# Casting the second half of the slot outputs on DVE, and an idle fill moved behind a product

## The chip, the core and the metric

The kernel runs on one core of one Trainium2 chip. A core has a matrix engine (TensorE, in the profile PE for its products and PEld for its weight loads), a vector engine (DVE), a scalar engine (ACT), GpSimd (POOL) and a sync engine (SP) that issues most transfers here. The engines run their own queues in order and wait for one another through semaphores. The metric is the device time of one execution in microseconds (us), and lower is better.

## The reference, cut to what matters

Sliding-window attention feeds a soft mixture of experts, and that one's output feeds a second mixture in which every token goes to one expert:

```python
attn = softmax(scale * q @ k.T, banded: 0 <= i - j < 64)
x = attn @ v                                  # 2304 tokens, 512 wide
logits = x @ phi                              # 32 slots, 4 for each of 8 experts
slot_input = softmax(logits, tokens).T @ x
slot_out[e] = relu(slot_input[e] @ w1[e]) @ w2[e]
x = softmax(logits, slots) @ slot_out
idx = argmax(cosine(x, expert_emb) / tau)     # one of 8 for each token
out[t] = gate[t] * (relu(x[t] @ w1b[idx[t]]) @ w2b[idx[t]])
```

## The kernel before

The program has four stages. Attention runs over 32 half head pairs (up to about 126 us in the trace). Then the 32 slots are finished, and their two layers run over the eight experts' weights (`layer1`, lines 707 to 711, and `layer2`, lines 726 to 730). Then the kernel finds which expert the first token goes to, loads that expert's weights from memory, and builds the routing values. The last stage, `ffn`, is the second mixture's two products for all tokens (172 to 283 us).

The change touches the seam between the second and the fourth stage. `layer2` leaves the 32 slot outputs in `so_ps`, one PSUM tile of 128 x 512 f32, which is one PSUM bank. Three copies read it: lines 843 and 844 cast its left and right 256 columns to bf16 into `sob`, and line 845 copies all of it to `so` in f32. All three stand on ACT.

From `sob` goes a short chain. Line 880 multiplies it, in four pieces of 128 columns, by `c0`, the first token's slot weights. Line 881 (DVE) copies the result to `k0b`. After three transposes (line 796, `trT(9)`) line 885 multiplies `k0b` by the expert embeddings, lines 886 and 887 (DVE) find the largest, and line 888 has SP load its number. With it `load_e` (lines 890 to 896) issues ten transfers, in turn a part of the expert's first matrix `w1e` and of its second `w2e`; the first part of `w1e` is 256 KB. From `so` line 903 makes a second set of products, whose results `esT` feed line 912 and so `gst`.

The copies of combining weights (`combT`, through `split_rows`, lines 697 to 703) write a rounded part `hi` on ACT and a rest on DVE.

The order of the work at the head of `ffn` is written out by hand in the string `SEQ` (line 9), one letter a step: `g` is `logits2` (line 923, six products of six token tiles each), `f` is `fill(still, 1)` (line 113), a product of the identity with itself into a PSUM tile that nobody reads, `U` is the step `u_part` (line 999, the first product with `w1e`; its result goes through `split_rows` into `ust`), `V` splits a part of `w2e` on DVE (lines 1031 and 1032) and `Q` is `up` for a block of 256 tokens (line 1019), which needs `ust`. Each engine gets its instructions in the order in which this string writes them.

Of the kernel before, what the change touches and what calls it, by code (L numbers as in the profile page):

```python
# [7 lines left out]

SEQ = 'ggfUgffVQPU2WR1PW0U3RQ0S1U3LP2SQWUL1Q3S0WPK23P2Q10ORGM012R3R'
FP32 = mybir.dt.float32  # L10
F32R = mybir.dt.float32r
BF16 = mybir.dt.bfloat16
# [7 lines left out]
def tile_kernel(ctx, tc, q, k, v, phi, w1, w2, emb, tau, w1b, w2b, out):  # L20
    nc = tc.nc
# [20 lines left out]
    def ps(tag):  # L42
        return pp.tile([128, 512], FP32, tag=tag, name=tag)
# [55 lines left out]
    with tc.manual_schedule():  # L99
# [580 lines left out]
        sob = cpool.tile([128, DM], BF16, name="sob")  # L680
# [144 lines left out]
        so_ps = ps("pv")  # L825
# [15 lines left out]
            layer2(t)  # L841
        pT = trT(6)
        nc.scalar.copy(out=sob[:, 0:256], in_=so_ps[:, 0:256])
        nc.scalar.copy(out=sob[:, 256:512], in_=so_ps[:, 256:512])
        nc.scalar.copy(out=so, in_=so_ps)
        mctx.close()

# [140 lines left out]
        def ffn(first):  # L988
# [26 lines left out]
            def up(nb, f0, n=2, dve=False):  # L1015
                a, l = hbuf[nb % 3]
                p = ps("s")[:, 0:256 * n]
                for i in range(n):
                    nc.tensor.matmul(p[:, 256 * i:256 * i + 256], lhsT=ucol[f0 + i], rhs=cTs[:, 256 * NBS[nb]:256 * NBS[nb] + 256], start=True, stop=True)  # L1019
                av = a[:, f0:f0 + n, :].rearrange("p f n -> p (f n)")  # L1020
                if dve:
                    nc.vector.tensor_scalar(out=av, in0=p, scalar1=0.0, scalar2=None, op0=ALU.max)
                else:
                    nc.scalar.activation(out=av, in_=p, func=ACTF.Relu)  # L1024
                nc.vector.scalar_tensor_tensor(out=l[:, f0:f0 + n, :].rearrange("p f n -> p (f n)"), in0=p, scalar=0.0,  # L1025
                                               in1=av.bitcast(FP32), op0=ALU.max, op1=ALU.subtract)
# [52 lines left out]
            def gates_now():  # L1079
# [6 lines left out]
                "P": lambda n: up(0, *CH[n]), "Q": lambda n: up(1, *CH[n]), "R": lambda n: up(2, *CH[n])}  # L1086
            for x in SEQ:
                if x in "0123":
# [65 lines left out]
```

## Time and profile before

| what | value |
|---|---|
| time, median of 3 runs | 291.96 us (291.24 to 292.74) |
| the profiled execution's own time | 290.68 us |
| its span in the trace | 289.0 us |
| TensorE products busy | 270.9 us, 94% |
| DVE / ACT / POOL busy | 169.4 / 123.7 / 60.4 us |
| chain of waits that ended last | PE 73%, ACT 9%, DVE 7%, DMA 3% of the span |
| mean granted TensorE clock | 0.995 |

The span is what the trace covers; the time also has what lies around it, 1.68 us here. A busy share says little by itself: what counts at a place is the chain of waits, which names for each stretch the engine that nobody else was waiting for.

### The profile page before, as it was taken

To read this page: it belongs to the slowest core of one execution; us is meant where nothing else is said; L and a number is where in the kernel's file an instruction comes from. 1 tells how busy PE (TensorE), PEld (TensorE's weight loads), DVE (VectorE), ACT (ScalarE), POOL (GpSimd) and SP (SyncE) were. 2 spreads that over 40 slices of the span, in tenths; PEclk is the share of its full clock that TensorE was granted. 3 is DMA by queue.
4 is the path that set the end of the run, shared out by engine and by line. 5 is a ranking of instruction groups with operands and counts; after the bars stand their busy time and mean duration, and the time that the engine had idled before them with its cause. 6 is when DMAs were issued, how large, how long until landed. Compare 5 with 4: busy or idle time off the path is not lost.

```text
span 289.0 us, 7506 instructions
## 1 busy us (share of the span) xinstructions
PE 270.9 (94%) x2846; PEld 209.0 (72%) x2846; DVE 169.4 (59%) x670; ACT 123.7 (43%) x328; POOL 60.4 (21%) x135
## 2 busy tenths in 40 slices
PE   7699989999989899899999999999999999999991
PEld 6477768877868787663342596788888888888891
DVE  4679877888778777553860256988333423233210
ACT  3785876687667867551310353324212112211100
POOL 5556434351423332003200005330000000000000
PEclk9999999999999999999999999999999999999998
DMA  5999999989999999999999089002220111010111
GB/s 134 282 226 282 280 280 285 297 255 282 271 335 277 283 299 334 387 366 385 390 387 344 6 229 354 3 0 92 81 47 36 39 61 49 36 39 36 74 43 35
DMA packets 53657, 57.23 MB, mean 198 GB/s; under 512 B 21490, under 2 KB 34034, under 8 KB 53618
## 3 DMA queue, kind: packets, MB, share of 16 engines
q1 hardware_dynamic: 53472, 56.70, 62.3%
q8 instruction: 24, 0.39, 0.6%
q14 instruction: 15, 0.12, 0.1%
q10 hardware_dynamic: 146, 0.02, 0.0%
HBM read 51.99 MB, written 4.72 MB: 196 GB/s over the span
## 4 chain that ended last, share of the span: by engine, by line
PE 73%; ACT 9%; DVE 7%; DMA 3%; SPq 2%; issue 2%; POOL 1%; POOLq 0%; ACTq 0%
PE et L1047 17%; PE pv L1047 17%; PE pv L325 5%; PE pv L729 5%; ACT sm L279 4%; PE tr L217 4%; PE s L1019 3%; PE tr L710 3%; PE s L710 2%; PE et L292 2%; ACT ets L298 2%; PE pv L382 2%; PE s L262 2%; DMA v<-in_v_dram 2%; DVE sm L278 2%
## 5 line engine op out<-in xcount | busy, mean ns | idle before, releaser
L279 ACT ACTIVATE sm<-sm,nm 128x128 f32<-128x128 f32 x144 | 47.3, 391 | 23.7 <-DVE nm L278 23.5
L1024 ACT ACTIVATE h<-s 128x512 fp32r<-128x512 f32 (+1 forms) x39 | 21.8, 565 | 68.7 <-PE s L1019 68.7
L1025 DVE SCALAR_TENSOR_TENSOR h<-s,h 128x512 fp32r<-128x512 f32 (+1 forms) x39 | 25.0, 648 | 40.0 <-ACT h L1024 39.9
L278 DVE CUSTOM_DVE_ANT_0 sm<-s,mask 128x128 f32<-128x128 f32 x144 | 34.1, 286 | 11.2 <-PE s L268 6.6
L1047 PE MATMUL et<-w2h,h 128*128 128x512 f32 (+1 forms) x160 | 37.4, 372 | 0.0
L1047 PE MATMUL pv<-w2h,h 128*128 128x512 f32 x144 | 36.8, 392 | 0.0
L1047 PEld LDWEIGHTS et<-w2h,h 128*128 128x128 f32 x160 | 27.1, 189 | 5.4 <-issue 0.8
L325 PE MATMUL pv<-v,ets 128*64 128x65 f32 x640 | 25.7, 226 | 4.6 <-ACT ets L298 3.3
L1047 PEld LDWEIGHTS pv<-w2h,h 128*128 128x128 f32 x144 | 26.1, 188 | 4.6
L325 PEld LDWEIGHTS pv<-v,ets 128*64 128x64 f32 x640 | 21.4, 137 | 11.1 <-ACT ets L298 8.2
L217 PE MATMUL tr<-ident,spare 128*128 128x128 f32 x120 | 19.4, 285 | 1.9 <-POOL spare L212 1.8
L186 POOL COPY v<-v 64x512 f32<-64x512 f32 x16 | 9.7, 609 | 51.3 <-DMA v<-in_v_dram 51.2
L298 ACT COPY ets<-et 128x512 f32<-128x512 f32 x32 | 18.3, 573 | 4.2 <-PE et L292 3.7
L212 POOL COPY spare<-spare 128x512 f32<-128x512 f32 x30 | 18.4, 613 | 8.1 <-PE tr L217 5.1
L1047 PE MATMUL et<-w2l,h 128*128 128x512 f32 (+1 forms) x80 | 19.4, 368 | 0.0
L292 PE MATMUL et<-ident,sm 128*128 128x128 f32 x128 | 19.3, 273 | 0.0
L1047 PE MATMUL pv<-w2l,h 128*128 128x512 f32 x72 | 19.1, 390 | 0.0
L312 DVE COPY xT<-tr 128x320 f32<-128x320 f32 (+1 forms) x31 | 14.0, 451 | 4.3 <-ACT ets L300 3.6
L337 DVE TENSOR_TENSOR x<-pv,rc 128x256 f32<-128x256 f32 (+1 forms) x32 | 15.7, 491 | 1.1
L217 PEld LDWEIGHTS tr<-ident,spare 128*128 128x128 f32 x120 | 12.6, 140 | 4.1 <-POOL spare L212 2.2
L1019 PEld LDWEIGHTS s<-cTs,ust 128*128 128x128 f32 x72 | 13.5, 190 | 2.8
L1047 PEld LDWEIGHTS et<-w2l,h 128*128 128x128 f32 x80 | 13.7, 189 | 2.1
(309 smaller groups left out, 432.5 us busy)
## 6 DMA issues: line engine op xcount, KB each, us to landing
w<-in_moe_w_dram SPq DMA_DIRECT2D x32, 1024.0 KB, 7.8
v<-in_v_dram SPq DMA_DIRECT2D x32, 128.0 KB, 4.8
spare<-in_q_dram SPq DMA_DIRECT2D x15, 256.0 KB, 7.2
spare<-in_k_dram SPq DMA_DIRECT2D x15, 256.0 KB, 6.4
out_dram<-acc SPq DMA_DIRECT2D x15, 256.0 KB, 2.0
w1e<-in_moe_w_dram SPq DMA_DIRECT2D x3, 512.0 KB
w2e<-in_moe_w_dram SPq DMA_DIRECT2D x3, 512.0 KB, 8.0
out_dram<-acc SPq DMA_DIRECT2D x6, 128.0 KB, 2.0
```

What stands on the lines that cost most here:

```text
L212: g.tensor_copy(out=perm[nm], in_=t)
L217: nc.tensor.transpose(po[:, r], perm[nm][:, r].rearrange("p h d -> p (h d)"), ident)
L278: nc.vector.tensor_tensor_reduce(out=sm[:, u], in0=s[h][:, a], in1=m, scale=-scale, scalar=3.0e38, op0=ALU.add, op1=ALU.min, accum_out=nm[ ...
L279: nc.scalar.activation(out=sm[:, u], in_=sm[:, u], func=ACTF.Exp, bias=nm[:, u:u + 1], scale=-1.0)
L292: nc.tensor.transpose(p[:, 128 * u:128 * u + 128], e[:, u, :], ident)
L298: nc.scalar.copy(out=o[:, 0:4], in_=p.rearrange("p (n h q) -> p n h q", n=4, h=2))
L325: nc.tensor.matmul(p[64 * par:64 * par + 64, a, h, :], lhsT=et[:, u, x, :], rhs=vt[:, sl, h, :], start=True, stop=True)
L337: nc.vector.tensor_tensor(out=x_tok[b, hp][:, js[0]:js[0] + nj].rearrange("p j (h d) -> p j h d", h=2), in0=p[:, :, :, 0:64], in1=rc[:, 0: ...
L1019: nc.tensor.matmul(p[:, 256 * i:256 * i + 256], lhsT=ucol[f0 + i], rhs=cTs[:, 256 * NBS[nb]:256 * NBS[nb] + 256], start=True, stop=True)
L1024: nc.scalar.activation(out=av, in_=p, func=ACTF.Relu)
L1025: nc.vector.scalar_tensor_tensor(out=l[:, f0:f0 + n, :].rearrange("p f n -> p (f n)"), in0=p, scalar=0.0, in1=av.bitcast(FP32), op0=ALU.ma ...
L1047: nc.tensor.matmul(dps[t], lhsT=x[:, fc, o:o + 128], rhs=w[fc // 4][:, fc % 4, o_:o_ + w_], start=fc == 0 and i == 0, stop=fc == FC - 1 an ...
```

## The change

Two edits. Line 844 goes from ACT to DVE: the cast of the right half of `so_ps` to bf16 becomes `nc.vector.tensor_copy`. And in `SEQ` the first `f` goes from ahead of the first `U` to behind it.

```diff
-SEQ = 'ggfUgffVQPU2WR1PW0U3RQ0S1U3LP2SQWUL1Q3S0WPK23P2Q10ORGM012R3R'
+SEQ = 'ggUfgffVQPU2WR1PW0U3RQ0S1U3LP2SQWUL1Q3S0WPK23P2Q10ORGM012R3R'
...
         nc.scalar.copy(out=sob[:, 0:256], in_=so_ps[:, 0:256])
-        nc.scalar.copy(out=sob[:, 256:512], in_=so_ps[:, 256:512])
+        nc.vector.tensor_copy(out=sob[:, 256:512], in_=so_ps[:, 256:512])
         nc.scalar.copy(out=so, in_=so_ps)
```

On ACT, at the end of `layer2` (`pv_2706` is the PSUM tile `so_ps`; a bracket names the engine whose semaphore the instruction waits for):

```order
 L702 CAST hi_2712<-et_2690 128x384 [waits PE_49]
 L843 CAST sob_2540<-pv_2706 128x256 [waits PE_49]
-L844 CAST sob_2540<-pv_2706 128x256
-L845 COPY so_2537<-pv_2706 128x512
-L702 CAST hi_2858<-et_2782 128x384 [waits DVE_49,PE_49]
+L845 COPY so_2537<-pv_2706 128x512 [waits DVE_49]
+L702 CAST hi_2858<-et_2782 128x384 [waits PE_49,Activation_49]
```

The second cast is gone from ACT, and the f32 copy of line 845 now waits for DVE, for which it did not wait.

On DVE, at the same place:

```order
 L790 TENSOR_TENSOR s16__2716<-s4__2600 128x384 [waits DMAHW5_49]
 L790 TENSOR_TENSOR s16__2716<-s4__2600 128x384
+L844 CAST sob_2540<-pv_2706 128x256 [waits Activation_49]
 L881 CAST k0b_2541<-tr_2816 128x4 [waits PE_49]
 L886 MAX g0_2794<-tr_2826 1x8 [waits DMAHW6_49,PE_49]
```

The cast stands ahead of `k0b` and waits for ACT; it has no wait for PE, the writer of `so_ps`.

On PE, at the first steps of `ffn` (`et_2930` is the third piece of `logits2`, `pv_2707` the tile of the fills):

```order
 L923 MATMUL s_2913<-gst_2799,cTs_2536 128x40 [waits PE_49]
 L923 MATMUL s_2913<-gst_2799,cTs_2536 128x40 x5
+L999 MATMUL tr_2921<-w1e_2812,esT_2800 128x128 [waits DMAHW5_49]
+L999 MATMUL tr_2921<-w1e_2812,esT_2800 128x128 x3
 L113 MATMUL pv_2707<-ident_67 128x128
-L999 MATMUL tr_2922<-w1e_2812,esT_2800 128x128 [waits DMAHW5_49]
-L999 MATMUL tr_2922<-w1e_2812,esT_2800 128x128 x3
 L923 MATMUL et_2930<-gst_2799,cTs_2536 128x40 [waits DVE_49]
 L923 MATMUL et_2930<-gst_2799,cTs_2536 128x40 x2
```

The product that waits for the transfer of `w1e` now stands directly behind the second piece of `logits2`, and the fill behind it. POOL's and SP's rows are the same in both kernels.

## Rows read from the trace of the kernel before

**Rows 1.** Chain that ended last, in order of time: start us, us, what.
```profile
163.34 0.20 PE tr L880 x2
163.54 0.39 PE et L796 x3
163.93 0.17 PE tr L885 x4
164.10 1.10 PE s L903 x8
...
168.72 0.31 PE pv L113 x2
169.03 0.89 PE tr L999 x8
...
170.50 0.54 PE pv L113 x4
171.04 0.23 PE s L1019 x2
```

**Rows 2.** Timeline, ACT: start us, us, engine, line, operation, out<-in, count [idle before <-releaser].
```profile
162.64 0.37 ACT L843 CAST sob<-pv 128x256 bf16<-128x256 f32 x1 [13.97 <-PE pv L729]
162.91 0.38 ACT L844 CAST sob<-pv 128x256 bf16<-128x256 f32 x1
163.18 0.60 ACT L845 COPY so<-pv 128x512 f32<-128x512 f32 x1
...
166.60 0.19 ACT L702 CAST hi<-tr 128x40 fp32r<-128x40 f32 x1 [1.07 <-PE tr L912]
```

**Rows 3.** Timeline, DVE.
```profile
163.58 0.16 DVE L881 CAST k0b<-tr 128x4 bf16<-128x4 f32 x1 [11.84 <-PE tr L880]
...
165.23 0.42 DVE L906 COPY esT<-s 128x256 f32<-128x256 f32 x1
...
166.83 0.26 DVE L703 SCALAR_TENSOR_TENSOR gst<-hi,misc,tr 128x40 fp32r<-128x40 f32 x1 [0.65 <-ACT hi L702]
...
170.26 0.35 DVE L703 SCALAR_TENSOR_TENSOR ust<-hi,misc,tr 128x128 fp32r<-128x128 f32 x1 [1.91 <-ACT hi L702]
```

**Rows 4.** Timeline, ACT and DVE in attention: two reads of one PSUM tile.
```profile
36.86 0.27 ACT L300 COPY ets<-tr 128x128 f32<-128x128 f32 x1
...
37.16 0.49 DVE L312 COPY xT<-tr 128x320 f32<-128x320 f32 x1 [0.82 <-ACT ets L300]
```

**Rows 5.** Line 300, who waited for it: us, times.
```profile
  DVE xT L312: 3.6, 5
```

**Rows 6.** Timeline, weight loads of PE.
```profile
163.34 0.11 PEld L880 LDWEIGHTS <-sob 128*128 128x128 bf16 x2 [0.16 <-ACT sob L844]
...
163.86 0.14 PEld L885 LDWEIGHTS <-k0b 128*1 128x1 bf16 x4 [0.17 <-DVE k0b L881]
...
164.03 0.97 PEld L903 LDWEIGHTS s<-sel,so 128*128 128x128 f32 x8
...
168.53 0.30 PEld L113 LDWEIGHTS pv<-ident 128*128 128x128 f32 x2
...
168.76 0.97 PEld L999 LDWEIGHTS tr<-w1e,esT 128*128 128x128 f32 x8
```

**Rows 7.** Timeline, SP's queue.
```profile
166.00 0.40 SPq L893 DMA_DIRECT2D w1e<-in_moe_w_dram  x1
```

**Rows 8.** Stretches: us, busy time of PE, PEld, DVE, ACT, POOL, granted clock, DMA share, GB/s.
```profile
168.00:168.25 0.25, 0.25 (x5) 0.25 (x4) 0.25 (x1) 0.17 (x1) 0.00 (x0) 1.00 1.28 150
168.25:168.50 0.25, 0.25 (x5) 0.25 (x4) 0.10 (x1) 0.20 (x1) 0.00 (x0) 1.00 0.32 49
```

**Rows 9.** Stretches, same columns: one early in attention, the first full one behind the last product.
```profile
10.00:12.00 2.00, 0.47 (x4) 0.47 (x5) 1.93 (x9) 1.98 (x7) 1.06 (x2) 1.00 1.12 228
...
287.00:289.00 2.00, 0.00 (x0) 0.00 (x0) 0.00 (x0) 0.00 (x0) 0.00 (x0) 0.50 0.05 12
```

## The prediction

> **What bounds the kernel now.** I read the chain of waits first, between the end of the slot layers and the second mixture's first products, because both edits lie there. It names PE for nearly every stretch [rows 1]. What the reader is to see is the one place where PE depends on the three copies of the slot outputs: line 880 gets its last two pieces at 163.34, right behind the second cast, which ends at 162.91 + 0.38 = 163.29 [rows 1, 2]. From there the chain runs without a gap worth naming through three transposes (0.39), line 885 (0.17) and line 903 (1.10). So a shift of that 163.34 is a shift of all that follows, one for one, and the number of the expert, which SP waits for, moves with it.
>
> The same rows show what does not bound. The casts overlap in the profile by 0.10 us (the first lasts to 163.01, the second starts at 162.91), so the second costs 0.28 us behind the first, not 0.38 [rows 2]. DVE has been idle for 11.84 us when line 881 comes [rows 3]: nothing of its own would hold up a cast there.
>
> At the second place the chain is PE's own work: a fill (0.31), the first product with the expert's weights (0.89), later two more fills (0.54), then line 1019 at 171.04 [rows 1]. Line 1019 needs `ust`, which DVE finishes at 170.26 + 0.35 = 170.61 [rows 3]. PE gets there 0.43 us later. It is not waiting for `ust`.
>
> **The cast on DVE.** It would help if the two halves were read side by side. The order of the instructions says otherwise: DVE's cast waits for ACT and has no wait for PE, though PE writes what it reads. It can be safe without one only if the ACT instruction it waits for is the first cast, which itself waits for PE. And line 845 on ACT now waits for DVE. The three reads of that one tile go in a row, with two handovers between engines, where ACT alone had its reads overlapped. The trace has the same pattern: line 312 on DVE reads columns 0 to 319 of a tile whose columns 384 to 511 line 300 reads on ACT, and it starts at 37.16, 0.03 behind the end of line 300 (36.86 + 0.27), after 0.82 of idling [rows 4]; five such waits add up to 3.6 us [rows 5].
>
> A rule of the Trainium skill says why: by "PSUM — Partial Sum Buffer", section "PSUM bank collisions raise a hardware error", two engines must not access one bank of the same partitions at once, reads included and whatever the columns, so that software has to keep them apart. The trace agrees, as far as rows 4 and 5 go. By that rule the sum is the one that follows; without it the edit would be the gain of the first rival.
>
> The sum. First cast ends 163.01. Handover from ACT to DVE: 0.04 (line 702 ends 166.60 + 0.19 = 166.79, line 703 starts 166.83) [rows 2, 3]. A DVE copy of 128 x 256 f32 from PSUM: 0.42, by line 906; none with bf16 out is in the trace, and I take this row because its shape and source are the same [rows 3]. So it ends at 163.47. Handover from DVE to a weight load on PE: 0.12 (line 881 ends 163.58 + 0.16 = 163.74, line 885 loads at 163.86) [rows 3, 6]. That makes 163.59 for the last two pieces of line 880, against 163.34: **+0.25 us**. Bounds: at the ACT cast's 0.38 in place of 0.42 it is +0.21; at the 0.49 of a 320 column copy [rows 4] and 0.03 for handovers that come out longer, +0.35. Below nothing it could go only if the reads overlapped, which is the first rival.
>
> Line 845 moves too. It starts behind DVE's cast, at 163.47 + 0.12 = 163.59 if this handover costs as much as the dearest one above, takes 0.60, and with 0.05 to PE (163.29 to 163.34 above) is ready at 164.24. Its reader, line 903, loaded at 164.03 and is itself 0.25 later, 164.28 [rows 2, 6]. So it stays covered, by 0.04, where it had been covered by 0.20 (163.83 against 164.03). A longer cast on DVE moves the copy and its reader alike; only a dearer handover to ACT breaks the cover, and then costs what it is over 0.16 (0.12 + 0.04). On DVE, line 881 is queued behind the new cast, but it needs the product with the cast's result anyway: nothing.
>
> SP issues the first transfer of the expert's weights at 166.00 [rows 7] and does so behind the same chain, so transfers and PE both move by 0.25.
>
> **The fill.** Nothing is removed: three fills stay three, so PE's own sum is unchanged. What moves is the first product, forward by one fill: its weights load at 168.53 in place of 168.76, on the old clock [rows 6]. It can't start before its part of `w1e` has landed. In the kernel before nothing waited for that, so the landing has no row; it is at or before 168.76, and a start at 168.53 costs PE between 0 and 168.76 - 168.53 = 0.23 us of waiting. The transfer rate drops from 150 to 49 GB/s in the quarter from 168.25 to 168.50 [rows 8], which I read as the end of the first part's data. I take 0, and keep 0.23 for the range. What the edit gives is an earlier `ust`, by the 0.31 of a fill. It was 0.43 us ahead of its reader already, so the gain is 0: the slack grows, and the next late thing is PE itself.
>
> **Sum.** +0.25 + 0 + 0 = +0.25 us, bounds +0.21 and +0.35 + 0.23 = +0.58. The profiled execution took 290.68 us and would take 290.93; the median of the runs is 291.96, 1.28 above it, and the forecast goes from there: **292.2 us**.
>
> **Rivals.**
> First, the casts do run side by side, as the edit's words have it. DVE then starts at 162.64 with ACT, ends 163.06, and PE loads at 163.18 against 163.34: -0.16, 291.8 us. For it: DVE is idle and the source is complete. Against it: the waits in the order, and rows 4 and 5.
>
> Second, the transfer takes over as what the first product waits for. PE then stands still for up to 0.23 us: with the casts as forecast +0.48, 292.4 us, more if the landing shifts from run to run. For it: the fill ahead was the one cover. Against it: the drop of the rate ahead of 168.53.
>
> Third, on the slower side: PE's two pauses, 0.25 longer than now ahead of line 880's second half and up to 0.23 long ahead of line 999, take the granted clock down from 2.4 to 1.2 GHz. Price: the work from the fill at 168.72 to the end of line 1019 at 171.04 + 0.23 = 171.27 [rows 1], 2.55 us, would take twice as long: with the casts 291.96 + 0.25 + 2.55 = 294.8 us, and more if the low grant lasts beyond that. The point from which it decides: between 10 and 12 PE was busy for 0.47 of 2 us, so idle for 1.53, and the grant stayed 1.00; it reads 0.50 from 287 to 289, where PE does nothing [rows 9]. The pauses here add under 0.5 us in sum, so this is unlikely.
>
> **How the numbers follow.** Forecast 0.76; casts side by side 0.08; the landing's wait 0.13; the clock 0.03. All but the last lie within 0.5% of 291.96 (1.46 us), which is about what a measurement of this kernel can tell from no change. The three runs shown spread from 0.72 below to 0.78 above their median, so a median of a few runs can miss by most of that either way: around 291.8 and 292.5, the ends of the first three cases, the range is 291.0 to 293.2. That spread also gives small chances of a reading past 0.5%: faster 0.04, same 0.89, slower 0.07, the clock's 0.03 among the last.
>
> **What the changed profile would show.** Right: line 844 on DVE starts some 0.04 behind the end of line 843 and lasts about 0.42; line 845 starts after it; the second pair of loads of line 880 comes some 0.95 us behind the start of line 843, not 0.70 as now (163.34 - 162.64); SP's first transfer of `w1e` lies about 3.6 us behind that start, not 3.36 as now (166.00 - 162.64); the first line 999 has no idle time ahead that a DMA ended; the granted clock reads 1.00 there. Wrong: line 844 starting with line 843 (first rival), an idle stretch of PE ahead of line 999 ended by the transfer (second), or a grant under 1.00 between 163 and 173 (third). A time outside 0.5% with all of these as forecast would mean that something I take as untouched, the transfers of attention above all, moved.

## The result

Over 20 runs each, the changed kernel took 294.83 us in the median and the kernel before 292.62; the ratio is 1.0071, with a 95% interval of 1.0047 to 1.0096. The forecast was 292.2 us, with a range of 291.0 to 293.2. So the change costs more than the forecast's 0.25 us, and the time lies outside the range. The ratios leave out the runs of a kernel that lie more than 1.5% above its fastest (one run of the kernel before took 381.29 us).

The ratio came out smaller each time after that. The changed kernel was timed four times more, each time beside the kernel before on one chip: 1.0028 (0.9987 to 1.0069), 1.0012 (0.9961 to 1.0063), 1.0031 (0.9985 to 1.0077) and 1.0022 (0.9970 to 1.0075), with 1 inside all four intervals. The unchanged kernel under another name gave 1.0030 (0.9993 to 1.0068), 1.0000 (0.9934 to 1.0065) and 0.9993 (0.9955 to 1.0030). The mean over all its 62 runs in which the clock is known is 294.54 us for the changed kernel and 292.96 us over the 161 of the unchanged one: a loss of some 1.6 us (1.2 to 2.0 on the four chips with both), of which the sections below place a part.

### The profile page after: what moved, and what is told of

It is laid out like the page before. It is cut to its first block, busy times and chain, and to the rows that moved or that the text cites. A ratio compares the mean times of both kernels' runs of the same rounds, so it can differ in the third digit from the quotient of the medians.

```text
span 291.2 us, 7506 instructions
## 1 busy us (share of the span) xinstructions
PE 271.4 (93%) x2846; PEld 209.0 (72%) x2846; DVE 170.4 (59%) x671; ACT 123.6 (42%) x327; POOL 59.9 (21%) x135
## 4 chain that ended last, share of the span: by engine, by line
PE 68%; DMA 10%; ACT 8%; DVE 6%; SPq 3%; issue 2%; POOL 1%; POOLq 0%; ACTq 0%
PE et L1047 17%; PE pv L1047 16%; PE pv L325 5%; DMA w<-in_moe_w_dram 5%; PE tr L217 4%; ACT sm L279 3%; PE s L1019 3%; PE et L292 3%; PE tr L710 3%; PE s L710 2%; PE s L262 2%; DMA w1e<-in_moe_w_dram 2%; ACT ets L298 2%; PE pv L382 2%; DMA v<-in_v_dram 2%
## 5 line engine op out<-in xcount | busy, mean ns | idle before, releaser
L1032 POOL TENSOR_TENSOR w2l<-w2e,w2h 128x1024 fp32r<-128x1024 f32 (+1 forms) x4 | 8.5, 2120 | 33.2 <-DVE w2h L1031 28.9
```

## The profile after

The profiled execution of the changed kernel took 293.27 us, with a span of 291.2 us against 289.0. First the place of the cast (timeline of ACT, DVE and the weight loads; start us, us, engine, line, operation, operands, count, idle time before and what ended it):

```profile
164.41 0.37 ACT L843 CAST sob<-pv 128x256 bf16<-128x256 f32 x1 [14.60 <-PE pv L729]
164.81 0.43 DVE L844 CAST sob<-pv 128x256 bf16<-128x256 f32 x1 [11.93 <-ACT sob L843]
164.83 0.11 PEld L880 LDWEIGHTS <-sob 128*128 128x128 bf16 x2 [0.25 <-ACT sob L843]
165.27 0.58 ACT L845 COPY so<-pv 128x512 f32<-128x512 f32 x1 [0.49 <-DVE sob L844]
165.29 0.11 PEld L880 LDWEIGHTS <-sob 128*128 128x128 bf16 x2 [0.35 <-DVE sob L844]
...
165.53 0.16 DVE L881 CAST k0b<-tr 128x4 bf16<-128x4 f32 x1 [0.30 <-PE tr L880]
...
165.81 0.14 PEld L885 LDWEIGHTS <-k0b 128*1 128x1 bf16 x4 [0.17 <-DVE k0b L881]
...
165.98 0.97 PEld L903 LDWEIGHTS s<-sel,so 128*128 128x128 f32 x8
...
167.95 0.41 SPq L893 DMA_DIRECT2D w1e<-in_moe_w_dram  x1
```

The casts do not run side by side: DVE starts 0.03 us behind the end of ACT's cast, ACT's f32 copy 0.03 behind the end of DVE's. The second pair of loads of line 880 comes 0.88 us behind the start of line 843 (165.29 - 164.41), where [rows 1, 2] have 0.70 for before. The cast alone therefore costs 0.18 us. The copy of line 845 ends at 165.85 and line 903 loads at 165.98, so the copy stays hidden. SP's first transfer of `w1e` lies 3.54 us behind the start of line 843 (forecast 3.6, before 3.36).

Then the first product with the expert's weights and the third part of `w1e` (the same timeline, and behind it PE's products at the third part):

```profile
169.18 1.49 PE L923 MATMUL s<-gst,cTs 128*128 128x40 f32 x12 [0.31 <-DVE gst L703]
...
170.64 0.97 PEld L999 LDWEIGHTS tr<-w1e,esT 128*128 128x128 f32 x8
...
172.90 0.48 PE L1019 MATMUL s<-cTs,ust 128*128 128x256 f32 x2
...
176.99 0.16 PEld L1003 LDWEIGHTS tr<-w1e,esT 128*32 128x32 f32 x8 [0.63 <-DMA w1e<-in_moe_w_dram]
176.99 0.64 PE L1003 MATMUL tr<-w1e,esT 128*32 128x256 f32 x8 [0.20 <-DMA w1e<-in_moe_w_dram]
```

The same products in the kernel before:

```profile
167.23 1.49 PE L923 MATMUL s<-gst,cTs 128*128 128x40 f32 x12 [0.31 <-DVE gst L703]
...
170.80 0.48 PE L1019 MATMUL s<-cTs,ust 128*128 128x256 f32 x2
...
171.11 1.10 PE L999 MATMUL tr<-w1e,esT 128*128 128x128 f32 x8
...
174.47 0.64 PE L1003 MATMUL tr<-w1e,esT 128*32 128x256 f32 x8
```

From the first product of line 923 to line 1019 it takes 3.72 us (172.90 - 169.18); in the kernel before 3.57, from 167.23 to 170.80. PE has the same work in between, so 0.15 us of it is new waiting, though the row of line 999 names none. The changed kernel's other three profiles without a fall of the clock (see below) have 3.72, 3.78 and 3.79 us there. From there to line 1003 it takes 4.09 us, before 3.67 (174.47 - 170.80): PE stands at the third part of `w1e`, for which it did not wait in the profile of before. The chain that ended last now runs through this transfer, and through the last weights of the slot layers (start us, us, what):

```profile
149.37 13.86 DMA w<-in_moe_w_dram
...
163.27 1.11 PE pv L729 x8
164.41 0.38 ACT sob L843
164.81 0.44 DVE sob L844
165.29 0.20 PE tr L880 x2
...
170.44 6.50 DMA w1e<-in_moe_w_dram
...
176.99 0.64 PE tr L1003 x8
```

Between the spans there are 2.2 us. Of them 0.75 lie at the seam: 0.18 at the cast, 0.15 ahead of line 1019, 0.42 behind it. The rest is older than the change: line 843 starts at 164.41 and not at 162.64, 1.77 later, after instructions that are the same in both kernels. In the other profiles it starts anywhere from 162.01 to 165.75, in copies of the unchanged kernel at 162.95, 163.69 and 164.03, so one pair of profiles can't say whose delay this is. From line 1003 to the last product it takes 108.6 us in both, and what follows the last product is 0.3 us shorter, which makes up the sum.

## The experiments

Theory H says that the handover between engines is all there is; theory W or L that PE now waits for transfers; theory C that PE's waits at the seam make the granted clock fall more often. In the texts put down before the runs, a ratio is the time over that of the kernel before.

**Each edit alone, both, and both with a fill on either side.** The two halves are the two hunks of the change. The fourth kernel adds one letter to the changed one:

```diff
-SEQ = 'ggUfgffVQPU2WR1PW0U3RQ0S1U3LP2SQWUL1Q3S0WPK23P2Q10ORGM012R3R'
+SEQ = 'ggfUfgffVQPU2WR1PW0U3RQ0S1U3LP2SQWUL1Q3S0WPK23P2Q10ORGM012R3R'
```

> Only the cast of the right half goes to DVE; the order string stays that of before. Theory H (handover between engines): the second pair of loads of line 880 comes about 0.88 us behind the start of line 843, as in the changed kernel's profile, where before it was 0.70; so +0.2 us in the profile at this place, and the time 1.0005 to 1.001 of before, which is no change. Theory C (the granted clock falls more often): C puts the loss to the fill, so here the ratio is 1.000 to 1.001 and the mean granted clock is that of before. If this edit alone carries the loss of some 2 us, the ratio is 1.005 or more, and both are wrong.

> Only the fill goes behind the first product with the expert's weights; both casts stay on ACT. Theory C: the product that waits for its transfer now stands where the fill kept PE busy, the granted clock falls in more runs, ratio 1.005 to 1.009 and the mean granted clock of the runs some 0.005 lower than where the fill is ahead. Theory W (the product waits for the transfer): PE idles up to 0.5 us ahead of line 999 by the transfer, ratio 1.000 to 1.002, the clock as before. Theory H: 1.000.

> The changed kernel once more, beside its two halves on the same chip. Measured: 1.0071 (1.0047 to 1.0096). All theories expect 1.005 to 1.009 here; if it comes out at 1.000 to 1.002, the loss hangs on the chip or the hour and not on the edits. If the halves are 1.000 each and this is 1.007, the edits act together, or the loss is in the placement of code or data.

> The changed kernel with one more fill ahead of the first product, so one stands on either side. Theory C: the fill ahead holds the clock again, the ratio falls to 1.001 to 1.003 (the extra fill itself costs 0.27 us of PE, 0.001, and the handover 0.2 us). Theory H or a cause in attention: the ratio stays at 1.006 to 1.010, the extra fill on top.

Measured: cast alone 1.0046 (0.9998 to 1.0093), fill alone 1.0009 (0.9962 to 1.0056), both 1.0028 (0.9987 to 1.0069), both with a fill more 1.0046 (1.0010 to 1.0082). The intervals are as wide as the differences, so the times decide little. The first form of C, which put the loss on the fill alone (1.005 to 1.009), is not borne out, nor is the 1.005 or more that all theories expected of both edits; the kernel with a fill more lies between what C and H expected. The profiles decide two things. From line 843 to the second pair of loads it takes 0.88 or 0.89 us in each profile with the cast on DVE and 0.69 or 0.70 in each without, here and in the runs below (but for the one with a longer wait): H holds for the cast. And with the fill alone line 923 to line 999 takes 1.34 us where it was 1.56: the product did start earlier by a fill there, and PE then stood at the third part of `w1e`. No time was lost ahead of line 1019 in this one profile (3.57 us, as before).

The profile of the cast alone showed something that no profile had shown. Stretches of it (us, busy time of PE, PEld, DVE, ACT and POOL with counts, granted clock, DMA share, GB/s):

```profile
162.60:166.00 3.40, 3.09 (x29) 2.40 (x28) 2.12 (x8) 2.08 (x5) 0.00 (x0) 1.00 0.00 0
166.00:169.40 3.40, 3.09 (x28) 2.89 (x28) 1.80 (x4) 1.77 (x5) 0.00 (x0) 1.00 0.61 158
169.40:172.80 3.40, 3.40 (x18) 3.40 (x18) 1.38 (x3) 0.62 (x2) 0.00 (x0) 0.50 0.98 297
172.80:176.20 3.40, 3.40 (x15) 3.11 (x14) 1.44 (x4) 0.92 (x3) 0.30 (x1) 0.50 1.04 368
176.20:180.00 3.80, 3.80 (x24) 2.60 (x24) 1.55 (x4) 1.66 (x5) 2.28 (x2) 0.99 1.02 358
```

The granted clock falls from 2.4 to 1.2 GHz for 6.8 us, and in it the second line 999 needs 1.91 us for its eight products (timeline below) where it needs 1.10 in the kernel before. From line 923 to line 1003 it takes 10.41 us, against 7.24 in the kernel before (174.47 - 167.23): such a fall costs 3.2 us. Two profiles of the unchanged kernel that have it (below) take 10.40 and 10.43.

```profile
167.37 1.49 PE L923 MATMUL s<-gst,cTs 128*128 128x40 f32 x12 [0.31 <-DVE gst L703]
...
172.89 1.91 PE L999 MATMUL tr<-w1e,esT 128*128 128x128 f32 x8
...
177.78 0.42 PE L1003 MATMUL tr<-w1e,esT 128*32 128x256 f32 x4
```

Seven of the 20 profiles have this fall. Each time it begins 1 to 2.5 us behind the start of line 923. Every run also gives its mean granted clock, so the time at half clock is 2 x (1 - clock) x span. In the profiles without the fall this is 1.2 to 7.0 us (the tail behind the last product, and in nine of the 20 profiles, with the fall at the seam or without, one of 3.4 us early in attention); in those with it 7.6 to 14.7. I count a run as one with the fall from 7.4 us on.

**A longer wait, and waits filled.** The first kernel has the cast on DVE, the order string of before, and two more copies ahead of the cast; the next two add two fills to the changed kernel and to the one before; the fourth is the fill alone once more, for its profile.

```diff
+        for _ in range(2):
+            nc.vector.tensor_copy(out=more[:, 1776:2032], in_=so_ps[:, 256:512])
         nc.vector.tensor_copy(out=sob[:, 256:512], in_=so_ps[:, 256:512])
```

```diff
-SEQ = 'gg...
+SEQ = 'fgg...
...
         for cc in range(4):
+            if cc == 2:
+                fill(still, 1)
             nc.tensor.matmul(p[:, cc:cc + 1], lhsT=sob[:, 128 * cc:128 * cc + 128], rhs=c0, start=True, stop=True)
```

> The cast on DVE alone, the order string of before, and two copies more of the same 256 columns on DVE (into scratch) ahead of it, so that the second pair of loads of line 880 comes some 0.8 us later still than with the cast alone and PE stands idle there for about 1.1 us and not 0.26. Theory H (the handover is all): the time is that of the cast alone plus 0.8 us. Theory C (the idle time of PE at this place makes the granted clock fall to half for 6.8 us some 6 us later, which costs 3.2 us): the share of runs with such a fall goes from about half to nearly all, the mean granted clock of the runs falls by 0.005 or more below the cast alone, and the time is 2 us or more above it, not 0.8.

> The changed kernel with two fills more: one between the two halves of line 880, where PE waits for DVE's cast, one ahead of the first piece of logits2, where PE waits 0.31 us for gst. Each costs what it is longer than the wait it fills, 0.0 to 0.1 us. Theory C: PE has no idle time left there, the runs with a fall of the clock at the seam get as few as in the kernel before or fewer (2 in 10), and the time falls by 0.5 to 1.5 us from the changed kernel's. Theory H: the time stays that of the changed kernel or rises by 0.1 us.

> The kernel before with the same two fills more. Theory C: where 7 of 35 runs of the kernel before had some 10 us or more at half clock, here 0 to 2 in 10 have; ratio 0.997 to 1.000. Theory H: no gain, ratio 1.000 to 1.001.

> The fill edit alone once more, for its profile. Theory L (with the fill behind, PE asks for the third part of w1e before it has landed): line 999 and line 1003 are ended by a DMA, and from the first line 923 to the first line 1003 it takes 7.7 to 8.0 us, as in the two profiles so far (7.84 in the changed kernel, 7.95 with the fill alone; 7.27 before). If the late landing was chance: 7.3 to 7.5.

Measured: longer wait 1.0067 (1.0011 to 1.0124), 7 of 11 runs with the fall; changed with waits filled 1.0052 (1.0011 to 1.0093), 3 of 11; before with waits filled 1.0013 (0.9962 to 1.0065), 1 of 11. In the profile of the longer wait PE idles 1.05 us ahead of the second half of line 880, and the fall is there:

```profile
166.62 0.20 PE L880 MATMUL tr<-c,sob 128*128 128x1 bf16 x2 [1.05 <-DVE sob L846]
```

Seven of 11 is not the "nearly all" that C expected of four times the wait. The profile of the fill alone had the fall too, and with it 10.80 us from line 923 to line 1003. A fall brings PE to the third part of `w1e` some 3 us later, so it tells nothing of the wait there. Ahead of it, at the first part, PE did wait for the transfer:

```profile
169.34 1.50 PE L999 MATMUL tr<-w1e,esT 128*128 128x128 f32 x8 [0.21 <-DMA w1e<-in_moe_w_dram]
```

**A copy of the unchanged kernel, and the three variants again.**

> The kernel before, unchanged, under another name: what the comparison says of no change. Ratio 1.000, interval within 0.005 either way; 2 to 3 runs in 10 with 7.4 us or more at half clock. From the start of line 843 to the first line 1003 11.8 us as in its first profile, if no fall of the clock lies there. If it comes out at 1.003 or more, as the kernel with only two fills added did in its undisturbed runs, a shift of that size is in the comparison and not in the edits.

> The changed kernel a third time, for the share of falls. Theory C: 7.4 us or more at half clock in 4 to 7 runs in 10 (17 of 32 so far, 14 of 62 for the kernel before), the other runs some 0.75 us above those of the kernel before (as line 843 to line 1003 in the profiles says), ratio 1.004 to 1.008. Without C: the same share as the kernel before.

> The fill edit alone. Theory C with the cast as its cause: 2 to 4 runs in 10 at 7.4 us or more of half clock, as before. Theory L (the third part of w1e is late whenever the fill stands behind the first product alone): it lands some 9.0 us behind the first issue, as in two of two profiles of this kernel (9.10, 9.16), and line 1003 waits for it; by chance alone 7.9 to 8.5, as in six of six profiles with a fill ahead.

> The cast edit alone. Theory C: 4 to 7 runs in 10 at 7.4 us or more of half clock (6 of 12 so far), the other runs 0.2 us above those of the kernel before; ratio 1.003 to 1.006. Theory H: the share as before, ratio 1.0005.

Measured: copy 1.0030 (0.9993 to 1.0068), both 1.0012 (0.9961 to 1.0063), fill 1.0001 (0.9960 to 1.0042), cast 1.0008 (0.9960 to 1.0056). C expected 1.004 to 1.008 for both and 1.003 to 1.006 for the cast: its shares of falls came (6 and 5 of 12), its times did not. The copy had the fall in 6 of 12 runs too, twice what was expected, and in its profile (stretches, columns as above):

```profile
166.40:169.80 3.40, 3.09 (x27) 2.88 (x27) 2.23 (x5) 1.59 (x6) 0.00 (x0) 1.00 0.48 135
169.80:173.20 3.40, 3.40 (x18) 3.40 (x18) 0.93 (x3) 0.79 (x3) 0.00 (x0) 0.50 0.87 257
```

So the unchanged kernel has it too. In the first profile of before the same stretch has the same busy time, and the grant stays:

```profile
166.00:169.40 3.40, 3.09 (x28) 2.88 (x28) 1.58 (x4) 1.77 (x5) 0.00 (x0) 1.00 0.69 178
169.40:172.80 3.40, 3.40 (x29) 3.29 (x28) 2.33 (x6) 1.55 (x5) 0.00 (x0) 1.00 1.03 258
```

PE is busy for 3.09 of the 3.40 us ahead in all three profiles, with a fall behind it in two. So PE's busy time ahead of the fall does not tell the one run from the other. The same copy also falls early in attention, right behind a stretch like that of [rows 9]:

```profile
10.00:12.00 2.00, 0.36 (x3) 0.36 (x4) 1.78 (x7) 1.96 (x7) 1.22 (x2) 1.00 1.12 211
12.00:14.00 2.00, 2.00 (x17) 1.67 (x19) 0.98 (x3) 1.41 (x4) 1.23 (x2) 0.70 1.00 312
```

The third run of the fill alone shows the wait at the first part, which I had put at 0, as the second did:

```profile
169.47 2.02 PE L999 MATMUL tr<-w1e,esT 128*128 128x128 f32 x8 [0.25 <-DMA w1e<-in_moe_w_dram]
```

But the cast alone, with the fill still ahead, waited as well:

```profile
168.91 1.49 PE L923 MATMUL s<-gst,cTs 128*128 128x40 f32 x12 [0.31 <-DVE gst L703]
...
170.72 0.97 PEld L999 LDWEIGHTS tr<-w1e,esT 128*128 128x128 f32 x8 [0.21 <-DMA w1e<-in_moe_w_dram]
...
172.76 0.49 PE L1019 MATMUL s<-cTs,ust 128*128 128x256 f32 x2
```

From line 923 to line 1019 it takes 3.85 us here, 0.28 more than in the kernel before with the same work. The landing moves from run to run by some tenths, and the fill ahead covers it in some runs (3.57 in two of two profiles of the unchanged kernel without a fall) and not in others.

**Waits filled, the change and the copy again.**

> The kernel before with the two fills in PE's waits at the seam, again. Theory C: 0 to 2 in 10 of the runs have 7.4 us or more at half clock (1 of 11 so far; 34 of 109 for the kernel before and its copy). Without C: 3 in 10 as without the fills. Ratio 0.998 to 1.002 either way, since the fills themselves cost 0.13 us from line 843 to line 1003.

> The changed kernel with the same two fills, again. Theory C: 1 to 3 in 10 of the runs have such a fall (3 of 11 so far), against 5 in 10 for the changed kernel (23 of 44); the time 0.5 to 1 us under the changed kernel's. Without C: no difference in the share.

> The changed kernel, for the share of falls and the ratio beside its covered twin on the same chip. Theory C: 4 to 6 in 10. If the three ratios so far (1.0071, 1.0028, 1.0012) are one value with noise, this is 1.002 to 1.007.

> The kernel before unchanged under another name, again. Its first time gave 1.003 (0.9993 to 1.0068) and 6 of 12 runs with a fall, so the comparison itself moves by some 0.003; here 0.997 to 1.003 and 3 in 10.

Measured: before with waits filled 1.0017 (0.9977 to 1.0057), no fall in 6 runs; changed with waits filled 1.0026 (0.9979 to 1.0072), 1 of 6; both 1.0031 (0.9985 to 1.0077), 2 of 6; copy 1.0000 (0.9934 to 1.0065), 4 of 6. Theory L, that the third part of `w1e` lands late whenever the fill stands behind, falls here: in the kernel before with waits filled, which has a fill ahead, PE waits for it longer than in any profile of the change.

```profile
178.09 0.64 PE L1003 MATMUL tr<-w1e,esT 128*32 128x256 f32 x8 [1.08 <-DMA w1e<-in_moe_w_dram]
```

In the changed kernel's third profile it did not wait there at all. The shares of falls came as C expected for the two kernels with waits filled, lower for the changed kernel (2 of 6) and higher for the copy.

Last the change and the copy as a pair:

> The changed kernel beside a copy of the unchanged one, both under names of their own. Theory C (the edits make the clock fall more often): 5 in 10 of the runs with 7.4 us or more at half clock, 2 us or more in the mean of all runs above the copy. Theory D (only what the trace shows at the seam: 0.18 for the cast, 0.15 and now and then more for the fill): 0.3 to 0.8 us above the copy in the runs without such a fall, and the share of falls no higher than the copy's.

> The copy of the unchanged kernel: 10 of 18 runs with such a fall so far, against 29 of 108 in the runs of the kernel before itself. Theory D: 4 to 6 in 10 again, so the share does not tell the kernels apart. Theory C: 2 to 3 in 10, and the 10 of 18 were chance. Ratio 1.000 to 1.003.

Measured, each against the kernel before on the same chip: both 1.0022 (0.9970 to 1.0075), median 294.77 us, 5 of 12 runs with the fall; copy 0.9993 (0.9955 to 1.0030), median 292.28 us, 2 of 12. The change lies 1.88 us above the copy in the mean of all runs, under C's 2, and 1.69 us in the mean of those without the fall, over D's 0.3 to 0.8: neither theory is met. In the copy's profile PE waited for the third part too:

```profile
176.37 0.64 PE L1003 MATMUL tr<-w1e,esT 128*32 128x256 f32 x8 [0.21 <-DMA w1e<-in_moe_w_dram]
```

All runs together, each counted (means in us; the error is the standard deviation over the root of the count):

| kernel | runs | mean of all | with the fall | mean of the others |
|---|---|---|---|---|
| before, as the reference of each comparison | 131 | 292.81 | 35 (27%) | 291.98 ± 0.12 |
| before, copy under another name | 30 | 293.58 | 12 (40%) | 292.21 ± 0.22 |
| fill alone | 25 | 293.50 | 7 (28%) | 292.59 ± 0.31 |
| cast alone | 24 | 293.83 | 11 (46%) | 292.47 ± 0.27 |
| both: the change | 62 | 294.54 | 30 (48%) | 293.17 ± 0.25 |
| both, fill on either side | 12 | 293.82 | 3 (25%) | 293.37 ± 0.22 |
| cast with a longer wait | 11 | 295.44 | 7 (64%) | 293.15 ± 0.21 |
| before, waits filled | 17 | 292.96 | 1 (6%) | 292.84 ± 0.33 |
| both, waits filled | 17 | 293.25 | 4 (24%) | 292.73 ± 0.33 |

Three things follow. Without the fall the change costs about 1.1 us (293.17 against 292.0). Of that the seam shows about half: from line 843 to the first line 1003 the four profiles of the changed kernel without a fall took 12.58, 12.57, 12.18 and 13.25 us, the two of the unchanged one 11.83 and 12.34, so 0.6 us more in the mean. Two parts of it stand in all four: 0.18 of the cast, and 0.15 to 0.22 ahead of line 1019. The rest is waiting for the later parts, which varies by more than it weighs and comes in the unchanged kernel too. The other half is not placed. Then the fall: 48% of the changed kernel's runs against 29% of the unchanged one's (47 of 161), which for equal shares would come about 1 time in 100; times 3 us this is 0.6 us. But the line at 7.4 us is thin: the clock is given to three decimals, a step of 0.6 us, and 7 of the changed kernel's 30 lie on the first step above the line. Counted from 8 us on it is 23 of 62 against 45 of 161, which equal shares give about 1 time in 5. And against the copies alone (12 of 30) the difference is not to be told from chance either. So it is not shown that the edits raise the share. Even the whole loss rests on the reference runs: against the copy timed beside it, the changed kernel's mean is 0.3 us longer, 0.6 shorter and 1.9 longer. Last, with fills in PE's waits the fall was rarer (5 of 34 runs, against 77 of 223 of the two kernels without; about 1 time in 35 by chance), but no time is won by it: the runs without a fall of before with its waits filled are 0.9 us longer, of which its two profiles without a fall at the seam show 0.13 in one and a late transfer in the other. No version here is shown to beat the kernel before.

## Why the prediction was wrong, point by point

- **The three reads go in a row.** Right, in every profile. The sum of this step was +0.25 us; it measured +0.18. The mis-sized term is the handover from DVE to a weight load on PE, taken at 0.12 from line 881 [rows 3, 6]. Behind the cast it is 0.05 (164.81 + 0.43 = 165.24 to 165.29), while behind line 881 it is again 0.12 in the same profile (165.53 + 0.16 = 165.69 to 165.81). Why the two differ, no run here shows. The cast's 0.42 was 0.43, and the cover of line 845 held. The signs named for this step came: line 844 behind line 843 by 0.03, and 3.54 us to SP's first transfer.
- **The rule on PSUM banks.** The trace agrees with the waits that the Trainium skill asks for in "PSUM — Partial Sum Buffer", section "PSUM bank collisions raise a hardware error": two readers of one bank, disjoint columns, one behind the other by 0.03 us. The first rival (side by side, 291.8 us) is out.
- **The fill costs 0.** Wrong, and the first step that failed: the wait of the first product for its part of `w1e`, taken at 0. I read the end of that part's data off a drop of the transfer rate [rows 8] and took the landing to be in time. In the changed kernel's four profiles without a fall, PE loses 0.15, 0.15, 0.21 and 0.22 us ahead of line 1019; with the fill alone it lost 0.21 and 0.25 at line 999 in two profiles, nothing in the third. So the second rival, at 0.13, had the mechanism, and its 0.23 the size. With the cast's 0.18 this makes 0.33 to 0.40 us, inside the bounds of the sum (+0.21 to +0.58). The sign that was to tell it, an idle stretch ahead of line 999 ended by the transfer, did not: that row has none in the changed kernel's profile, with 0.15 lost. And the 0.23 held for that product alone. It left out the parts that follow: the second and third part of `w1e` land just as PE asks for them (0.42 us in the changed kernel's profile), and a landing late by some tenths goes straight into the time, in the kernel before as well.
- **The falling clock.** This is most of what carries the time out of the range, and the second step that failed. I priced it at 2.55 us and gave it 0.03, because the pauses are short and PE had idled 1.53 of 2 us early in attention at a grant of 1.00 [rows 9]. But by the mean clock the unchanged kernel has the fall in 29% of its runs (28% counted from 8 us), so it needed no new pause; the one profile of before, which has none, could not show that. And the idle time was no point of decision: in a copy's profile the grant falls right behind such a stretch of attention, and at the seam it falls behind PE busy for 3.09 of 3.40 us. Of the changed kernel's 20 runs in the result 12 have the fall (8, if counted from 8 us); the eight under the line of 7.4 us have a mean of 293.28 us, just past the edge of the range. The price was near: 3.2 us. What decides whether the clock falls stays open.
- **The range.** Its width, and the 291.96 under the forecast, came from three runs that spread from 291.24 to 292.74. Twenty runs of the same kernel have a median of 292.62, so 0.66 us of the 2.63 by which the forecast missed were there before any step of it. The runs with a known clock lie on two levels, with and without the fall, some 3 us apart. With the change the median shifts when the share of falls nears one half, by more than any term of my sum. The range should have reached to a run with the fall, 295. The prediction's last sentence also came in part: in the one profile after, line 843 starts 1.77 us later, behind a transfer of the slot weights, which the edits do not touch.

## What to carry to other kernels

Here a second engine beside the first one gained nothing, because both read one PSUM bank: look in the order of the waits whether the reads are put in a row, and count the lost overlap of back-to-back instructions on one engine (0.10 us here) beside the handovers. A fill that stands ahead of a product which waits for a transfer can cover a late landing (here not every time), so the landing's spread, not its one value, belongs in the sum. And before a few tenths are forecast, look at the mean granted clock of many runs and not at the profile alone, and time a copy of the unchanged kernel under another name: here that copy moved by up to 0.3%.

## What the runs showed of the hardware

The granted clock fell from 2.4 to 1.2 GHz for 6.8 us in seven of 20 profiles. In two of them PE was busy nine tenths of the 3.4 us ahead, and in a third profile with the same busy time the clock did not fall. By the mean clock it fell in some runs of every kernel here. Eight products of line 999 took 1.91 us in it and not 1.10, and 3.2 us were lost. A handover between ACT and DVE cost 0.03 us either way; from DVE to a weight load on PE it was 0.05 behind a copy of 256 columns and 0.12 behind one of 4. The third part of `w1e`, 512 KB, kept PE waiting 0 to 1.08 us at line 1003 among the profiles without a fall, and 0 and 0.21 in two of the unchanged program.
